# Reordering the first 20 microseconds of a fused layernorm, GLU and state-space kernel: warm-up products first, the first group's turns between grad's products, and turned x copied on ScalarE

## The chip, the cores and the metric

The kernel runs on one core of one Trainium2 chip. The metric is the device time of one execution in microseconds (us), median over several executions.

Engines: PE is TensorE (matmuls), PEld its weight loads, DVE is VectorE, ACT is ScalarE, POOL is GpSimd, SP is SyncE. PSUM is the memory that PE writes its products to and DVE and ACT read them from (in the timelines below the tiles `ps_...`: PE's rows write them, rows such as `xT<-ps_mm` on DVE and ACT read them).

The order in which each engine works through its instructions is fixed when the program is built: a scheduler orders the whole program, engine by engine, and at run time each engine takes its list from the front. So moving one call in the source can move other instructions on other engines too.

## The reference, cut to what matters

```python
# forward; the kernel returns its output and the gradients of all inputs for grad_out
x = A_u                                   # [1, 2048, 576], bfloat16
xn = layernorm(x)
gate = xn @ W_gate; up = xn @ W_up        # W: [576, 4608]
h = relu(gate) * up
out = x + S4(xn, A, B, C, log_dt, Dskip) + h @ W_down
# out, and the vector-Jacobian product of (x, A_*, B_*, C_*, log_dt, Dskip, W_*) with grad_out
```

The kernel goes through the 4608 hidden columns in 12 chunks of 384, each chunk in three units of 128 (`ft` = 0, 1, 2), and through the 2048 rows in four groups of 512 (`sg` = 0 to 3). The first chunk also normalises x. After it, the work of the state-space part (S4) is woven in between the chunks' products.

## The kernel before

Warm-up. PE multiplies an identity by itself 60 times, meant to run before any input has landed, so that PE is at its full rate when real work comes:

```python
    ps = g.psum_s4.tile([P, 512], F32, name="ps_s4")
    for i in range(WARM):                               # 60
        nc.tensor.matmul(ps[:, 0:P], lhsT=g.ident_bf[:], rhs=g.ident_bf[:], start=True, stop=True)
    nc.scalar.copy(warm[:], ps[:, 0:1])
```

Normalising one group and turning it (a "turn" is a 128x128 transpose on PE; five of them fill one PSUM tile, and one copy takes it to SBUF):

```python
def ln_group(g, pools, sg, x4, gT):
    for j in range(JS):                                 # 4 row blocks: statistics on DVE
        # ... 2 x bn_stats and 1 x bn_aggr of x4[:, j]
    # ... mean and rounding on DVE, square root (sdb) on ACT, sdf and rinv on DVE
    for j in range(JS):                                 # x - mean: DVE and ACT in turn
        # ...
    for j in range(JS):
        nc.vector.tensor_scalar(xn4[:, j, 0:D], x4[:, j, :], g.rinv[...], None, op0=ALU.mult)
        pt = g.psum_mm.tile([P, 512], F32, name="ps_mm")[:]...
        for k in range(NK):                             # 5 turns
            nc.tensor.transpose(out=pt[:, k, :], in_=xn4[:, j, k * P:(k + 1) * P], identity=g.ident_bf[:])
        (nc.vector.tensor_copy if j % 2 == 0 else nc.scalar.copy)(xT[:, :, j * P:(j + 1) * P], pt[:, 0:NK, :])
    # ... stores of xT and xn
```

The products of grad for group 0 (three bundles of five matmuls, `first`), one unit, and the order of the first chunk:

```python
    def first(self, gT):
        for ft in range(FTC):                           # 3
            ps = g.psum_mm.tile([P, 512], F32, name="ps_mm")
            # ... 5 matmuls of gT into ps
            nc.scalar.copy(self.dh0[ft], ps[:])

    def a_unit(self, c, sg, ft, turns=()):
        # gate: 5 matmuls of xT; up: 5 of xT; grad: 5 of gT (group 0 of chunk 0 has it from first)
        nc.scalar.activation(rg, ps_g[:], ACT.Relu)                                     # reads gate's PSUM tile
        nc.vector.scalar_tensor_tensor(upm, rg, 0.0, ps_u[:], op0=ALU.is_gt, op1=ALU.mult)  # reads up's
        # ... products on DVE

    # gen, chunk 0:
                xs = [ln_load(g, self.ln_sb, 0, 2)]
                # ... loads: wd[2], gT of group 0, wd[0], wd[1], x of group 1, wf, x of groups 2 and 3
                self.first(gT)
                self.X[(0, 0)] = ln(0, xs[0], gT)
                for ft in range(FTC):
                    yield from self.a_unit(0, 0, ft)
                self.X[(0, 1)] = ln(1, xs[1], self.load_gT(1))
                # ... then units of group 1, turns of group 2, products with wf, and so on
```

All of these tiles come from one PSUM pool, `psum_mm`, with five tiles; a second pool, `psum_s4`, belongs to the S4 part.

Of the kernel before, what the change touches and what calls it, by code (L numbers as in the profile page):

```python
# [10 lines left out]
F32 = mybir.dt.float32  # L11
# [3 lines left out]
P = 128  # L15
# [8 lines left out]
NK = 5  # L24
DP = NK * P
Fc = 384
FTC = Fc // P
# [43 lines left out]
def dchunks():  # L71
    return [(k, k * P, min(P, D - k * P)) for k in range(NK)]
# [4 lines left out]
def make_consts(g):  # L77
    nc, consts = g.nc, g.consts
    g.ident_bf = consts.tile([P, P], BF16, name="ident_bf")
    make_identity(nc, g.ident_bf[:])  # L80
    g.hpcol = consts.tile([P, 1], F32, name="hpcol")
    nc.vector.memset(g.hpcol[:], math.pi / 2)
    warm = consts.tile([P, 1], F32, name="warm")
    nc.scalar.activation(warm[:], g.hpcol[:], ACT.Sqrt)
    ps = g.psum_s4.tile([P, 512], F32, name="ps_s4")
    for i in range(WARM):
        nc.tensor.matmul(ps[:, 0:P], lhsT=g.ident_bf[:], rhs=g.ident_bf[:], start=True, stop=True)
    nc.scalar.copy(warm[:], ps[:, 0:1])
    g.rinv = consts.tile([P, ST], F32, name="rinv")
    g.dsk_acc = consts.tile([P, NK, NSG], F32, name="dsk_acc")  # L90

# [15 lines left out]
def ln_load(g, sb, sg, pieces=1):  # L107
    nc = g.nc
    x4 = sb.tile([P, JS, D], BF16, name="x4")
    n = JS // pieces  # L110
    for j in range(0, JS, n):
        nc.sync.dma_start(x4[:, j:j + n], g.x_v[:, sg * JS + j:sg * JS + j + n, :])
    return x4

def ln_group(g, pools, sg, x4, gT):
    nc, bal = g.nc, g.bal
    sb, small = pools
    t0 = sg * JS
    mv = small.tile([P, JS, nc.vector.BN_AGGR_DIM], F32, name="mv")
    for j in range(JS):  # L120
        stats = small.tile([P, 2, nc.vector.BN_STATS_DIM], F32, name="stats")
        for s in range(2):
            nc.vector.bn_stats(out=stats[:, s, :], in_=x4[:, j, s * DH:(s + 1) * DH])
        nc.vector.bn_aggr(out=mv[:, j, :], in_=stats[:])
    mvb = small.tile([P, JS, 2], BF16, name="mvb")
    nc.vector.tensor_copy(mvb[:], mv[:])
    veb = small.tile([P, JS], BF16, name="veb")
    nc.vector.tensor_scalar(veb[:], mvb[:, :, 1], 1e-5, None, op0=ALU.add)
    sdb = small.tile([P, JS], BF16, name="sdb")
    nc.scalar.activation(sdb[:], veb[:], ACT.Sqrt)  # L130
    neg = small.tile([P, JS], F32, name="neg")
    nc.vector.tensor_scalar(neg[:], mvb[:, :, 0], -1.0, None, op0=ALU.mult)
    sdf = small.tile([P, JS], F32, name="sdf")
    nc.vector.tensor_copy(sdf[:], sdb[:])
    nc.vector.reciprocal(g.rinv[:, t0:t0 + JS], sdf[:])
    xn4 = sb.tile([P, JS, DP], BF16, name="xn4")
    nc.gpsimd.memset(xn4[:, :, D:DP], 0.0)
    xT = g.xtp.tile([P, NK, JS * P], BF16, name="xT")
    for j in range(JS):
        if j % 2 == 0:  # L140
            nc.vector.tensor_scalar(x4[:, j, :], x4[:, j, :], neg[:, j:j + 1], None, op0=ALU.add)
        else:
            nc.scalar.activation(x4[:, j, :], x4[:, j, :], ACT.Identity, bias=neg[:, j:j + 1])
    for j in range(JS):
        nc.vector.tensor_scalar(xn4[:, j, 0:D], x4[:, j, :], g.rinv[:, t0 + j:t0 + j + 1], None, op0=ALU.mult)
        pt = g.psum_mm.tile([P, 512], F32, name="ps_mm")[:].bitcast(BF16).rearrange("p (k t) -> p k t", t=P)
        for k in range(NK):
            nc.tensor.transpose(out=pt[:, k, :], in_=xn4[:, j, k * P:(k + 1) * P], identity=g.ident_bf[:])
        (nc.vector.tensor_copy if j % 2 == 0 else nc.scalar.copy)(xT[:, :, j * P:(j + 1) * P], pt[:, 0:NK, :])
    nc.sync.dma_start(g.xT_dram[sg], xT[:])  # L150
    nc.sync.dma_start(g.xn_dram[:, t0:t0 + JS, :], xn4[:, :, 0:D])
    for k, d0, dsz in dchunks():
        nc.sync.dma_start(g.xs_dram[k][:, t0:t0 + JS, :], xn4[:, :, d0:d0 + dsz])
    bal.add(d=6.5, a=2.5)
    return xT, gT

class Ffn:
# [38 lines left out]
        nc.sync.dma_start(xT[:], g.xT_dram[sg])  # L196
        self.X[(c, sg)] = (xT, self.load_gT(sg))

    def first(self, gT):
        g, nc = self.g, self.g.nc  # L200
        for ft in range(FTC):
            ps = g.psum_mm.tile([P, 512], F32, name="ps_mm")
            for k in range(NK):
                nc.tensor.matmul(ps[:], lhsT=self.wd[2][:, k, ft * P:(ft + 1) * P], rhs=gT[:, k, :], start=(k == 0), stop=(k == NK - 1))
            self.dh0[ft] = self.op.tile([P, 2, D], BF16, name="osx")[:].rearrange("p i d -> p (i d)")[:, 0:JS * P]
            nc.scalar.copy(self.dh0[ft], ps[:])
# [158 lines left out]
    def gen(self, ln, final):  # L365
        g, lu = self.g, FTC - 1
        for c in range(NFC):
            if c == 0:
                xs = [ln_load(g, self.ln_sb, 0, 2)]
                self.load_wd(0, (2,))  # L370
                gT = self.load_gT(0)
                self.load_wd(0, (0, 1))
                xs.append(ln_load(g, self.ln_sb, 1))
                self.load_wf(0, g.nc.sync)
                xs += [ln_load(g, self.ln_sb, sg) for sg in (2, 3)]
                self.first(gT)
                self.X[(0, 0)] = ln(0, xs[0], gT)
                for ft in range(FTC):
                    yield from self.a_unit(0, 0, ft)
                self.X[(0, 1)] = ln(1, xs[1], self.load_gT(1))  # L380
            else:
                self.load_wd(c)
                self.load_x(c, 0)
                for j in range(JS):
                    yield from self.outdx(c - 1, NSG - 1, j, turns=[(c - 1, NSG - 1, lu)] if j == 0 else ())
                for q in range(4):
                    yield from self.dw_down(c - 1, q)
                self.load_wf(c)
                yield from self.a_unit(c, 0, 0)
                for i in range(4):  # L390
                    yield from self.dw_gu(c - 1, i)
                    if i % 2 == 1 and 1 + i // 2 < FTC:
                        yield from self.a_unit(c, 0, 1 + i // 2)
                yield from self.dw_left(c - 1)
                for ft in range(3, FTC):
                    yield from self.a_unit(c, 0, ft)
                if c == 1:
                    self.dskip(0)
                elif c == 2:
                    self.dskip_out()  # L400
            if c > 0:
                self.load_x(c, 1)
            late = [(c, 0, ft) for ft in range(FTC)]
            for sg in range(1, NSG):
                todo = list(range(JS))
                for ft in range(FTC):
                    n = max(1, (len(late) + lu - 1) // lu) if ft < lu else len(late)
                    turns, late = late[:n], late[n:]
                    yield from self.a_unit(c, sg, ft, turns)
                    if c == 1 and ft == lu:  # L410
                        self.dskip(sg)
                    late.append((c, sg, ft))
                    if c == 0 and ft == 0 and sg < 3:
                        self.X[(0, sg + 1)] = ln(sg + 1, xs[sg + 1], self.load_gT(sg + 1))
                    for j in todo[:JS // lu] if ft < lu - 1 else todo:
                        if ft == lu:
                            break
                        args = (c, sg - 1, j)
                        if c == NFC - 1:
                            yield "last"  # L420
                            args += (final,)
                        yield from self.outdx(*args)
                    todo = todo[JS // lu:]
                if sg < NSG - 1 and c > 0:
                    self.load_x(c, sg + 1)
                if sg == NSG - 2:
                    self.rows(c, 0)
        c = NFC - 1
        for j in range(JS):
            yield from self.outdx(c, NSG - 1, j, final, turns=[(c, NSG - 1, lu)] if j == 0 else ())  # L430
        for i in range(4):
            yield from self.dw_down(c, i)
        for i in range(4):
            yield from self.dw_gu(c, i)
        yield from self.dw_left(c)
# [784 lines left out]
```

## Time and profile before

| | before |
|---|---|
| time, median of 6 executions | 1805.13 us (1802.98 to 1808.24) |
| PE busy, share of the span | 96% |
| first product of gate (group 0) | 20.46 us |
| first product of gate (group 1) | 29.75 us |
| first product with wf (`ps_mm<-wf,T`) | 35.70 us |
| first product of the S4 part (`<-sig,Sx`) | 96.03 us |

The last two rows are landmarks, read from PE's timeline.

The line of busy times on the page of the kernel before (us, share of the span, instructions):

```profile
PE 1724.5 (96%) x16449; PEld 1188.0 (66%) x16449; DVE 1309.8 (73%) x2867; ACT 1187.4 (66%) x2736; POOL 204.3 (11%) x246
```

PE is what binds: only work or waits taken out of PE's own row can shorten the run by much, and there is 4% of waits in all.

PE's timeline in the kernel before. Columns: start, busy time in us, engine, source line, operation, output and inputs, shape, count; in brackets how long PE had been idle and what released it:

```profile
8.69 0.58 PE L204 MATMUL ps_mm<-gT,wd_152 128*128 128x512 bf16 x1 [8.69 <-DMA gT<-in_gT_dram]
9.07 5.68 PE L87 MATMUL ps_s_75<-ident_bf 128*128 128x128 bf16 x60
14.59 3.19 PE L204 MATMUL ps_mm<-gT,wd_152 128*128 128x512 bf16 x14
17.61 1.28 PE L148 MATMUL ps_mm<-ident_bf,xn_266 128*128 128x128 bf16 x20
20.46 1.24 PE L235 MATMUL ps_mm<-xT,wd_150 128*128 128x512 bf16 x5 [1.57 <-ACT xT L149]
...
29.75 1.25 PE L235 MATMUL ps_mm<-xT,wd_150 128*128 128x512 bf16 x5 [1.53 <-DVE xT L149]
...
35.70 4.57 PE L288 MATMUL ps_mm<-wf,T 128*128 128x288 bf16 x36
```

Three things are to be seen. PE does nothing until 8.69, when gT lands. The 60 warm-up products then run in front of 14 of the 15 products of grad, when real products are already there to run. (PE's rate isn't up yet. The clock column of the profile shows 1.00, so this slow beginning isn't in that column.) Between the turns (17.61) and gate's first product (20.46) PE waits 1.57 us for the turned x.

The windows of the kernel before: for each stretch the width in us and each engine's busy time, in brackets the instructions that touch the stretch; PEclk is the granted clock of PE, 1.00 is full:

```profile
core 0: us, PE busy (x) PEld busy (x) DVE busy (x) ACT busy (x) POOL busy (x), PEclk, DMA share, GB/s
...
18.00:21.00 3.00, 1.43 (x19) 1.10 (x17) 2.98 (x9) 2.41 (x5) 0.00 (x0) 1.00 0.38 135
21.00:24.00 3.00, 3.00 (x16) 1.36 (x14) 2.89 (x11) 0.70 (x2) 0.00 (x0) 1.00 0.89 290
24.00:27.00 3.00, 3.00 (x17) 1.35 (x16) 3.00 (x9) 1.09 (x2) 0.00 (x0) 1.00 0.94 210
27.00:30.00 3.00, 1.47 (x23) 1.18 (x22) 3.00 (x11) 1.69 (x4) 0.00 (x0) 1.00 0.95 294
```

### The profile page before, as it was taken

The numbers are of one execution on the slowest core, as the hardware profiler recorded it, in microseconds if no ns is written. First come the engines' busy times: TensorE is split into PE (matmuls) and PEld (weight loads), VectorE is DVE, ScalarE is ACT, GpSimd is POOL, SyncE is SP. The second block draws the span as 40 slices with busy tenths as digits, with TensorE's granted clock in tenths as the row PEclk, the third lists the DMA queues.
The fourth block names the chain that finished last, engine by engine and source line by source line (L and its number), as shares of the span: only waits on it lengthen the run. The fifth ranks groups of instructions, "written<-read, shape, count | busy, mean of one in ns | idle before, by whom it ended". The sixth has DMA issues, their size and how long they took to land. (4 is left out here: it accounts for less than half of the span.)

```text
span 1804.8 us, 42093 instructions
## 1 busy us (share of the span) xinstructions
PE 1724.5 (96%) x16449; PEld 1188.0 (66%) x16449; DVE 1309.8 (73%) x2867; ACT 1187.4 (66%) x2736; POOL 204.3 (11%) x246
## 2 busy tenths in 40 slices
PE   7989989999999999999999999999999998999998
PEld 5665557667566666766756766766676675576676
DVE  7565885677888788668777889889888863872551
ACT  5875874686577578568468657748857745864651
POOL 0200011012022012011102101101101100110000
PEclk9999999999999999999999999999999999999999
DMA  8799989679568566766857856756666578995873
GB/s 293 264 331 301 332 238 284 193 181 252 163 137 202 179 178 146 227 183 153 225 157 183 230 167 153 214 171 156 174 179 151 111 211 262 249 288 156 266 241 100
DMA packets 239004, 373.30 MB, mean 207 GB/s; under 512 B 49490, under 2 KB 153428, under 8 KB 237268
## 3 DMA queue, kind: packets, MB, share of 16 engines
q1 hardware_dynamic: 212836, 304.09, 51.9%
q0 software_dynamic: 24384, 51.92, 18.5%
q10 hardware_dynamic: 1584, 14.60, 2.3%
q8 instruction: 129, 2.11, 0.5%
q14 instruction: 71, 0.58, 0.1%
HBM read 233.10 MB, written 137.43 MB: 205 GB/s over the span
## 5 line engine op out<-in xcount | busy, mean ns | idle before, releaser
L288 PE MATMUL ps_mm<-wf,T 128*128 128x288 bf16 x3456 | 486.7, 289 | 6.9 <-DVE T L247 2.5
L288 PEld LDWEIGHTS <-T 128*128 128x128 bf16 x3456 | 325.9, 99 | 94.8 <-issue 10.1
L67 ACT CAST osx<-ps_mm 128x288 bf16<-128x288 f32 x682 | 261.2, 432 | 58.0 <-PE ps_mm L288 54.1
L301 POOL DMA_DIRECT2D acc_dram<-osx x160 | 138.0, 862 | 1054.6 <-ACT osx L67 652.3
L341 PEld LDWEIGHTS <-rows 128*128 128x128 bf16 x1536 | 145.9, 98 | 94.0 <-issue 1.8
L245 DVE SCALAR_TENSOR_TENSOR rg<-rg,ps_mm 128x512 bf16<-128x512 bf16 x144 | 98.2, 682 | 120.9 <-PE ps_mm L235 91.4
L261 PEld LDWEIGHTS <-T 128*128 128x128 bf16 x1728 | 127.6, 98 | 88.3 <-DVE T L247 7.1
L235 PE MATMUL ps_mm<-xT,wd_150 128*128 128x512 bf16 x720 | 180.0, 379 | 5.0 <-DMA xT<-xT_dram 1.7
L235 PE MATMUL ps_mm<-xT,wd_151 128*128 128x512 bf16 x720 | 180.0, 379 | 0.0
L235 PE MATMUL ps_mm<-gT,wd_152 128*128 128x512 bf16 x705 | 176.4, 379 | 0.7 <-DMA gT<-in_gT_dram 0.7
L261 PE MATMUL ps_mm<-ident_bf,T 128*128 128x128 bf16 x1728 | 157.8, 220 | 7.8 <-DVE T L247 4.3
L325 PE MATMUL ps_mm<-rows,hN 128*128 128x144 bf16 x2304 | 159.1, 227 | 0.0
L325 PEld LDWEIGHTS <-hN 128*128 128x128 bf16 x2304 | 148.5, 98 | 8.1 <-issue 5.5
L67 ACT CAST obw<-ps_mm 128x384 bf16<-128x384 f32 x103 | 49.1, 477 | 140.7 <-PE ps_mm L341 105.9
L341 PE MATMUL ps_mm<-duN,rows 128*128 128x384 bf16 x768 | 136.3, 326 | 0.0
L341 PE MATMUL ps_mm<-dgN,rows 128*128 128x384 bf16 x768 | 136.1, 326 | 0.0
L244 ACT ACTIVATE rg<-ps_mm 128x512 bf16<-128x512 f32 x144 | 87.1, 605 | 55.6 <-PE ps_mm L235 55.0
L67 ACT CAST dhb<-ps_mm 128x512 bf16<-128x512 f32 x141 | 83.7, 594 | 56.1 <-PE ps_mm L235 54.4
L252 DVE TENSOR_TENSOR T<-dhb,rg 128x1024 bf16<-128x1024 bf16 x141 | 98.5, 698 | 26.4 <-ACT dhb L67 26.3
L235 PEld LDWEIGHTS <-wd_150 128*128 128x128 bf16 x720 | 66.3, 98 | 65.1 <-issue 5.1
L235 PEld LDWEIGHTS <-wd_151 128*128 128x128 bf16 x720 | 65.0, 98 | 60.1 <-issue 2.1
L235 PEld LDWEIGHTS <-wd_152 128*128 128x128 bf16 x705 | 63.3, 98 | 57.9 <-issue 1.2
(2504 smaller groups left out, 3047.0 us busy)
## 6 DMA issues: line engine op xcount, KB each, us to landing
acc_dram<-osx POOLq DMA_DIRECT2D x176, 288.0 KB, 5.0
gT<-in_gT_dram SPq DMA_DIRECT2D x48, 640.0 KB, 6.1
xT<-xT_dram SPq DMA_DIRECT2D x44, 640.0 KB, 6.0
rows<-in_gq_dram SPq DMA_DIRECT2D x48, 576.0 KB, 4.0
wf<-in_Wf_dram ACTq DMA_DIRECT2D x11, 1296.0 KB, 8.5
ex_dram<-exs SPq DMA_DIRECT2D x36, 320.0 KB, 4.4
ex<-ex_dram SPq DMA_DIRECT2D x36, 320.0 KB, 3.7
out_dram<-obw SPq DMA_DIRECT2D x96, 96.0 KB, 2.5
```

Source lines behind the costliest of these rows:

```text
L67: self.nc.scalar.copy(out, in_)
L235: nc.tensor.matmul(ps[:], lhsT=w[:, k, fs], rhs=rhs[:, k, :], start=(k == 0), stop=(k == NK - 1))
L244: nc.scalar.activation(rg, ps_g[:], ACT.Relu)
L245: nc.vector.scalar_tensor_tensor(upm, rg, 0.0, ps_u[:], op0=ALU.is_gt, op1=ALU.mult)
L252: nc.vector.tensor_tensor(T[:, 1:3], dhb.unsqueeze(1).to_broadcast([P, 2, JS * P]), ru[:], op=ALU.mult)
L261: nc.tensor.transpose(out=pt[:, j, :], in_=src[:, j * P:(j + 1) * P], identity=g.ident_bf[:])
L288: nc.tensor.matmul(ps[:, cs], lhsT=lt, rhs=rh, start=(i == 0), stop=(i == len(mms) - 1))
L301: nc.gpsimd.dma_start(g.acc_dram[:, t, :, :], o[:], accum_op=ALU.add)
L325: nc.tensor.matmul(ps[:, ft * 144:(ft + 1) * 144], lhsT=self.hN[:, st, ft * P:(ft + 1) * P], rhs=gq[:, st, :], start=(st == 0), stop=(st = ...
L341: nc.tensor.matmul(ps[:, :Fc], lhsT=xs[:, st, 0:P], rhs=src[:, st, :], start=(st == 0), stop=(st == ST - 1))
```

## The change

The intent: use the idle time before 8.69 for the warm-up, let the turns of group 0 run as soon as x is normalised, move group 1's turns forward by one unit, and take the copies of turned x off DVE.

```diff
-    ps = g.psum_s4.tile([P, 512], F32, name="ps_s4")
+    g.ps0 = g.psum_mm.tile([P, 512], F32, name="ps_mm")
     for i in range(WARM):
-        nc.tensor.matmul(ps[:, 0:P], lhsT=g.ident_bf[:], rhs=g.ident_bf[:], start=True, stop=True)
-    nc.scalar.copy(warm[:], ps[:, 0:1])
+        nc.tensor.matmul(g.ps0[:, 0:P], lhsT=g.ident_bf[:], rhs=g.ident_bf[:], start=True, stop=True)
@@ ln_group
-        (nc.vector.tensor_copy if j % 2 == 0 else nc.scalar.copy)(xT[:, :, j * P:(j + 1) * P], pt[:, 0:NK, :])
+        (nc.vector.tensor_copy if False else nc.scalar.copy)(xT[:, :, j * P:(j + 1) * P], pt[:, 0:NK, :])
@@ first
-    def first(self, gT):
+    def first(self, gT, fts):
-        for ft in range(FTC):
-            ps = g.psum_mm.tile([P, 512], F32, name="ps_mm")
+        for ft in fts:
+            ps = g.psum_mm.tile([P, 512], F32, name="ps_mm") if ft > 0 else g.ps0
@@ gen, chunk 0
-                self.first(gT)
+                self.first(gT, (0,))
                 self.X[(0, 0)] = ln(0, xs[0], gT)
+                self.first(gT, range(1, FTC))
                 for ft in range(FTC):
+                    if ft == FTC - 1:
+                        self.X[(0, 1)] = ln(1, xs[1], self.load_gT(1))
                     yield from self.a_unit(0, 0, ft)
-                self.X[(0, 1)] = ln(1, xs[1], self.load_gT(1))
```

The warm-up writes the PSUM tile that the first real product writes next. So nothing can put that product ahead of the warm-up any more.

## The prediction

> **What bounds the kernel.** PE. The page's busy table has PE 1724.5 us of 1804.8 (96%), DVE 73%, ACT 66%, clock full throughout. So a change gains only what it takes out of PE's order or waits; this one touches the first 60 us.
>
> **The opening, from the timeline.** PE waits until 8.69 us for gT (PE's largest single wait, 8.7 us). The first product of grad runs, then, although written first in the program, the 60 warm-up products: 9.07 to 14.59. In the windows table they run 12 per us (about 83 ns each) until about 13.5, then 25 to 30 per us. The other 14 products of grad follow (14.59 to 17.6, 216 ns each), the 20 turns of group 0 (17.6 to 18.9, 60 to 65 ns each), a wait of 1.57 us for the turned x, and gate and up begin at 20.46. The wait is ACT's: casts of grad (0.58 us) and biases of group 1 (0.76, 0.79) stand between its copies of xT (0.70).
>
> **What the change does.**
> 1. The warm-up shares a PSUM tile with the first real product, so it must come first. ident_bf is ready at 1.6 us; 60 products at 83 ns fill 1.8 to about 6.8, inside the wait for gT. Off the critical path: about -5.5 us.
> 2. Group 0's turns come after five products of grad; normalised x is ready at 9.70 (DVE timeline). Estimate: five products 8.7 to 9.8, turns to 11.1, ten products to 13.2. Four copies on ACT (about 0.65 each in a row) and a cast end near 13.1. Gate and up start at 13.2 instead of 20.46. With 1: -7.2 us.
> 3. Group 1's turns move before the last gate/up unit: the 1.53 us wait before 29.75 can go, but xn of group 1 may not be ready by 17.5 (its x lands at 12.46): net -0.5 us.
> 4. Copies: eight go from DVE (0.48) to ACT (0.70): ACT +5.6, DVE -3.9 us. ACT is 97% busy in 30 to 40 us, so groups 2 and 3 may stall PE: +0.5 us.
> 5. DMA is full from 8.7 to 18 us (about 400 GB/s) and 90 to 100% busy from 25 to 60. gT of group 1 and later tiles are wanted 8 us earlier against the same bytes: +1 us.
> 6. Clock: [...] the rate doubles some 5 us after the first product. [...]
>
> The rest is the same work in nearly the same order; static reordering may move it a few us either way.
>
> **Prediction.** 1805.1 - 7.7 + 2 = about 1799.4 us, 8 in 10 within 1794.5 to 1804.5. Faster by over 2%: 0.01; within 2%: 0.98; slower: 0.01.
>
> **What would show it.** Warm-ups end before 8 us; first gate product near 13.2, unit (group 1, first) near 22 instead of 29.75; PE busy down by only 0 to 1 us, with the gain in idle before the first gate product; DVE busy -4, ACT +5.
>
> **What would make it wrong.** The scheduler reordering later stages; the lead eaten by DMA waits (gT, xT) before 100 us; cold products at the start.

How the sum was made: steps 1 to 3 give -7.2 - 0.5 = -7.7 us, and the +2 was 0.5 (step 4) + 1 (step 5) + 0.5 for the clock (step 6), which gave 1799.4. The clock's term and its reason are cut from step 6, because no trace or run of this case shows the reason; without the term the sum is 1805.1 - 7.7 + 1.5 = 1798.9. "Clock full throughout" was read from the page, whose clock row has 9 (90% or more) in all 40 slices; over that whole run the mean granted clock is 0.992. "Cold products" means products at PE's slow rate, as the first warm-up products above.

## More of the kernel before

DVE is nearly full from 18 us (2.89 to 3.00 of 3), and in 27 to 30 it's busy 3.00 of 3 us while PE isn't.

Landmarks come from one profile of each kernel. The landing of gT, a load at the very start, varies and moves what follows it, so differences of less than about 1 us between two landmarks shouldn't be leaned on.

## The result, and the profile after

| | before | after |
|---|---|---|
| time, median | 1803.49 us of 20 (1797.64 to 1813.49) | 1802.98 us of 10 (1800.88 to 1813.23) |
| gate, group 0 | 20.46 us | 12.95 us |
| gate, group 1 | 29.75 us | 27.35 us |
| first product with wf | 35.70 us | 34.60 us |
| first product of S4 | 96.03 us | 95.34 us |

The ratio is 1.0002, 95% interval 0.9985 to 1.0019: the same. A ratio here is the mean time of one kernel's fast runs over the mean of the other's in the same rounds, so it isn't quite the ratio of the medians in the table (and the 6 executions of the first table are among these 20).

So 7.51 us were won at the gate, as predicted, and 0.7 us were left at 95 us. Nearly all of it was given back between 12.95 and 34.60.

The line of busy times of the kernel after:

```profile
PE 1726.3 (96%) x16449; PEld 1186.8 (66%) x16449; DVE 1307.1 (72%) x2859; ACT 1191.5 (66%) x2743; POOL 205.0 (11%) x246
```

PE's busy time rose by 1.8 us although the work is the same; DVE fell by 2.7 and ACT rose by 4.1, somewhat less than the predicted 4 and 5.

PE's timeline in the kernel after:

```profile
1.66 4.79 PE L87 MATMUL ps_mm<-ident_bf 128*128 128x128 bf16 x60 [1.66 <-POOL ident_bf masks.py:199]
8.60 1.24 PE L203 MATMUL ps_mm<-gT,wd_151 128*128 128x512 bf16 x5 [2.15 <-DMA gT<-in_gT_dram]
...
12.95 1.24 PE L234 MATMUL ps_mm<-xT,wd_149 128*128 128x512 bf16 x5
...
16.19 1.24 PE L234 MATMUL ps_mm<-xT,wd_150 128*128 128x512 bf16 x5
19.31 0.73 PE L147 MATMUL ps_mm<-ident_bf,xn_376 128*128 128x128 bf16 x10 [1.87 <-ACT rg L243]
21.17 1.02 PE L147 MATMUL ps_mm<-ident_bf,xn_376 128*128 128x128 bf16 x10 [1.13 <-DVE rg L244]
23.13 2.29 PE L234 MATMUL ps_mm<-xT,wd_149 128*128 128x512 bf16 x5 [0.94 <-DVE rg L244]
25.22 2.34 PE L234 MATMUL ps_mm<-xT,wd_150 128*128 128x512 bf16 x5
27.35 1.69 PE L234 MATMUL ps_mm<-xT,wd_149 128*128 128x512 bf16 x5
...
32.96 1.59 PE L147 MATMUL ps_mm<-ident_bf,xn_532 128*128 128x128 bf16 x20 [0.42 <-DVE xn_532 L144]
34.60 4.88 PE L287 MATMUL ps_mm<-wf,T 128*128 128x288 bf16 x36
```

To be read against the one of before: the warm-up is at 1.66 and done before gT lands at 8.60; gate begins at 12.95. Then PE waits three times (1.87 and 1.13 us at the turns of group 1, and 0.94 before the last unit). The named releasers are `rg`, that is, the instructions of the units that read PSUM (`relu` on ACT, L243, and the product on DVE, L244). And the five-product bundles at 23.13 and 25.22 are busy for 2.29 and 2.34 us where such a bundle took 1.24 at 16.19.

The windows of the kernel after tell why the bundles are slow (columns as above):

```profile
core 0: us, PE busy (x) PEld busy (x) DVE busy (x) ACT busy (x) POOL busy (x), PEclk, DMA share, GB/s
...
18.00:21.00 3.00, 0.73 (x10) 0.66 (x11) 3.00 (x12) 2.47 (x5) 0.00 (x0) 1.00 1.05 386
21.00:24.00 3.00, 1.89 (x13) 1.17 (x13) 3.00 (x9) 1.37 (x3) 0.00 (x0) 0.57 1.08 227
24.00:27.00 3.00, 3.00 (x9) 1.04 (x8) 1.97 (x7) 0.60 (x1) 0.00 (x0) 0.50 1.00 324
27.00:30.00 3.00, 3.00 (x19) 1.45 (x18) 2.33 (x9) 0.87 (x2) 0.00 (x0) 0.79 1.10 351
```

From 21 us on the granted clock is 0.57, 0.50 and 0.79. In finer slices it is exactly one half from about 21.4 to 28.2 us. In the profile of before it is 1.00 in all the windows shown above. Note also DVE: 3.00 of 3 in 21 to 24, and 1.97 and 2.33 in the two windows of slow products, since then DVE waits for PE (1.70 us in one piece, until 27.66).

What DVE and ACT did before that, from the timeline of all engines in the kernel after (a few of its rows):

```profile
17.66 0.46 DVE L122 BATCH_NORM_STATS2 stats<-x_209 128x6 f32<-128x288 bf16 x1 [0.66 <-DMA x_209<-in_A_u_dram]
...
18.20 1.07 ACT L243 ACTIVATE rg<-ps_mm 128x512 bf16<-128x512 f32 x2
...
18.89 1.20 DVE L144 TENSOR_SCALAR xn_376<-x_206,rinv 128x576 bf16<-128x576 bf16 x4
...
20.44 0.68 DVE L244 SCALAR_TENSOR_TENSOR rg<-rg,ps_mm 128x512 bf16<-128x512 bf16 x1
...
22.39 0.69 DVE L244 SCALAR_TENSOR_TENSOR rg<-rg,ps_mm 128x512 bf16<-128x512 bf16 x1
```

At 17.66 DVE takes up a statistics instruction on x_209, which is group 2's x; it waited 0.66 us for that to land. Group 1's normalised x (`xn_376`), for which PE has been waiting since 17.4, comes behind it, at 18.89 (the first of its four blocks is done at about 19.3, the last at 20.09). The trace puts PE's first wait down to a relu on ACT that ends at 19.27, but that is the same moment, and in e11 below, where the turns need no tile of the units, the same wait ends with the normalised x. So the first wait counts as one for DVE. The two DVE products that free the units' PSUM tiles come at 20.44 and 22.39, and it is those that release the second half of the turns (21.17) and the last unit (23.13).

The ledger from gate's first product to wf's first product: 35.70 - 20.46 = 15.24 us before, 34.60 - 12.95 = 21.65 us after, 6.41 more. Of this:

- waits: 1.87 + 1.13 + 0.94 + 0.42 = 4.36 against 1.53, so 2.83 more;
- units at half clock: the 15 products from 23.13 to 28.88 took 5.75 us; at full clock they take 15 x 0.216 = 3.24 (in this trace such products start 216 ns apart at full clock and 427 ns at half); so 2.51 more;
- group 1's turns: 0.73 + 1.02 against 1.28, so 0.47 more, of which about 0.3 is half clock (in e5 the second half takes 0.72 at full clock);
- the rest, 0.6 us, is spread: 0.27 of it in group 2's turns (1.59 against 1.32).

The first product of S4, PE's timeline before:

```profile
96.03 0.29 PE L609 MATMUL ps_s_1560<-sig,Sx 128*128 128x288 bf16 x1
```

and after:

```profile
95.34 0.29 PE L610 MATMUL ps_s_1558<-sig,Sx 128*128 128x288 bf16 x1
```

The lead of 1.1 us at 34.60 is 0.7 us here. So it isn't in later stages that most of the gain goes; of 7.5 us, 6.4 are gone before 35 us.

### The profile page after: what moved, and what is told of

It is laid out like the page before. It is cut to its first block, busy times and chain, and to the rows that moved or that the text cites. A ratio compares the mean times of both kernels' runs of the same rounds, so it can differ in the third digit from the quotient of the medians.

```text
span 1803.0 us, 42088 instructions
## 1 busy us (share of the span) xinstructions
PE 1726.3 (96%) x16449; PEld 1186.8 (66%) x16449; DVE 1307.1 (72%) x2859; ACT 1191.5 (66%) x2743; POOL 205.0 (11%) x246
## 5 line engine op out<-in xcount | busy, mean ns | idle before, releaser
L244 DVE SCALAR_TENSOR_TENSOR rg<-rg,ps_mm 128x512 bf16<-128x512 bf16 x144 | 98.3, 682 | 120.3 <-PE ps_mm L234 89.9
L243 ACT ACTIVATE rg<-ps_mm 128x512 bf16<-128x512 f32 x144 | 87.1, 605 | 53.7 <-PE ps_mm L234 53.1
```

## The experiments

Theories on the table, in words: the new waits of group 1's turns took the gain, and half the clock came from them; the copies on ACT took it; VectorE's work for later groups held group 1 back; the landings of x in memory order did; the units' PSUM tiles, being held, did. Twelve kernels ran (the record has no number 10). "wf" is the start of the first product with wf, "S4" that of the first S4 product.

| kernel | gate | wf | S4 | half clock in 8 to 35 us | median us | ratio to before (95%) |
|---|---|---|---|---|---|---|
| before | 20.46 | 35.70 | 96.03 | none | 1803.49 | 1 |
| after | 12.95 | 34.60 | 95.34 | 21.4 to 28.2 | 1802.98 | 1.0002 (0.9985 to 1.0019) |
| e1_move_undone | 13.70 | 34.52 | 95.24 | 24.8 to 31.6 | 1802.59 | 0.9994 (0.9975 to 1.0013) |
| e2_dve_copies | 17.98 | 34.19 | 94.52 | 9.9 to 13.3 | 1800.52 | 0.9987 (0.9964 to 1.0011) |
| e3_warm_only | 19.75 | 37.40 | 97.72 | 16.9 to 23.7 | 1805.12 | 1.0012 (0.9989 to 1.0034) |
| e4_fill | 13.64 | 36.86 | 97.59 | none | 1805.86 | 1.0014 (0.9994 to 1.0034) |
| e5_no_stats | 12.95 | 34.52 | 95.26 | 22.6 to 29.4 | 1806.77 | 0.9988 (0.9956 to 1.0019) |
| e6_fused | 13.16 | 32.65 | 93.07 | none | 1801.03 | 0.9969 (0.9947 to 0.9990) |
| e7_x3_late | 13.41 | 34.06 | 97.26 | 21.0 to 27.8 | 1806.46 | 0.9998 (0.9979 to 1.0016) |
| e8_before_x3_late | 20.64 | 36.10 | 99.38 | none | 1810.58 | 1.0022 (0.9997 to 1.0047) |
| e9_x2_before_wf | 12.95 | 34.74 | 95.47 | 22.6 to 29.4 | 1803.46 | 1.0001 (0.9976 to 1.0025) |
| e11_turns_s4 | 12.94 | 32.34 | 92.80 | 20.2 to 23.6 | 1801.30 | 0.9991 (0.9968 to 1.0013) |
| e12_combined | 12.48 | 35.88 | 96.38 | 25.3 to 32.1 | 1804.14 | 1.0002 (0.9980 to 1.0025) |
| e13_gT_early | 13.80 | 32.69 | 93.15 | none | 1798.69 | 0.9987 (0.9963 to 1.0011) |

No total is over 2% from before, and all but one interval (that of e6, which isn't a valid kernel) include 1. The landmarks are what tells the theories apart; the totals can only confirm.

### e1: the move of group 1's turns undone

Against the kernel after:

```diff
                 for ft in range(FTC):
-                    if ft == FTC - 1:
-                        self.X[(0, 1)] = ln(1, xs[1], self.load_gT(1))
                     yield from self.a_unit(0, 0, ft)
+                self.X[(0, 1)] = ln(1, xs[1], self.load_gT(1))
```

> The changed kernel with one part undone: group 1's turns are called again after the three units of group 0. Theory W (waits): the lead of 7.5 us that the changed kernel has at its first gate product (12.95 against 20.46) is spent by group 1's turns, which stand in PE's order before the last unit at a time when their x is not normalised and PSUM is not free (1.87 + 1.13 + 0.94 us of PE waits), and by the half clock that these waits bring on (21.6 to 28.2 us, about 2.5 us). W expects here: last unit follows at once (by 19.0), first gate product of group 1 at 22 to 24 (changed: 27.35, before: 29.75), no half clock between 15 and 30, first product with wf at 29 to 31.5 (changed: 34.60), and a total 3 to 6 us below before at equal clock. Rival C (copies): the loss is the turned x of all groups on ACT; then nothing is regained. Rival D (later stage sets the pace): the lead is taken back by other waits before 60 us, so the first L-product of the fourth stage at about 95 us stays within 1 us of 95.3.

Measured: gate at 13.70 (gT landed later, at 9.35), the turns of group 1 at 21.26 and 23.22 after waits of 0.43 and 1.25 us for the same DVE products, then 1.77 us for the copied xT, and half clock from 24.8 on. wf starts at 34.52, against 34.60. My expectation that the lead would be kept failed. The waits move behind the units and are as long; the place of the turns isn't the cause by itself.

### e2: copies alternate between DVE and ACT again

Against the kernel after:

```diff
-        (nc.vector.tensor_copy if False else nc.scalar.copy)(xT[:, :, j * P:(j + 1) * P], pt[:, 0:NK, :])
+        (nc.vector.tensor_copy if j % 2 == 0 else nc.scalar.copy)(xT[:, :, j * P:(j + 1) * P], pt[:, 0:NK, :])
```

> The changed kernel with the copies of turned x alternating between DVE and ACT again, in all four groups; warm-up and moves stay. Rival C expects the lead back: first wf product near 30 and 4 us less in all. Theory W expects the waits at group 1's turns as in the changed kernel (first gate product of group 1 within 1.5 us of 27.35) and a total within 2 us of it.

Measured: a DVE copy of xT then stands behind group 1's statistics, PE waits 1.97 us for it, and gate starts at 17.98, five us later than in the kernel after. wf nevertheless starts 0.4 us earlier (34.19). Not all of these five us are the copies': gT landed 1.24 us later in this profile (9.84 against 8.60), and the first products of grad and group 0's turns ran at half clock (9.9 to 13.3, a loss of up to 1.7 us), after PE had idled 2.37 us behind the early warm-up. So the copies on ACT bring about 2 us at the gate, and giving them up doesn't bring the lead back at wf. What they cost there isn't told by the 0.4 us, since e2 also lost less to half clock than the kernel after. The main lesson is another: five us at the gate were worth nothing at wf. What sets wf's time is not when gate begins.

### e3: the warm-up alone moved ahead

Against the kernel before:

```diff
-    ps = g.psum_s4.tile([P, 512], F32, name="ps_s4")
+    g.ps0 = g.psum_mm.tile([P, 512], F32, name="ps_mm")
     for i in range(WARM):
-        nc.tensor.matmul(ps[:, 0:P], lhsT=g.ident_bf[:], rhs=g.ident_bf[:], start=True, stop=True)
-    nc.scalar.copy(warm[:], ps[:, 0:1])
+        nc.tensor.matmul(g.ps0[:, 0:P], lhsT=g.ident_bf[:], rhs=g.ident_bf[:], start=True, stop=True)
@@ first
-            ps = g.psum_mm.tile([P, 512], F32, name="ps_mm")
+            ps = g.psum_mm.tile([P, 512], F32, name="ps_mm") if ft > 0 else g.ps0
```

> The kernel before with the warm-up alone forced ahead (shared PSUM tile), nothing moved, copies alternating. Theory W: first gate product at 14 to 15 us (5.5 to 6.5 us ahead of before), group 1's first gate product at 23 to 24.5 (before: 29.75), total 3 to 6 us below before at equal clock. Rival D: lead gone by 60 us, total as before. Rival K (clock): an earlier warm-up by itself lets the array fall to half clock in 15 to 30 us; then the granted clock there is under 0.9 here too.

Rows of the timeline of all engines in e3 (columns as before):

```profile
12.63 1.18 DVE L122 BATCH_NORM_STATS2 stats<-x 128x6 f32<-128x288 bf16 x3 [2.82 <-DMA x<-in_A_u_dram]
...
18.11 0.88 DVE L148 COPY xT<-ps_mm 128x640 bf16<-128x640 bf16 x2
18.43 1.27 ACT L148 COPY xT<-ps_mm 128x640 bf16<-128x640 bf16 x2
...
19.75 0.59 PE L234 MATMUL ps_mm<-xT,wd 128*128 128x512 bf16 x1 [6.40 <-ACT xT L148]
```

PE was done with the turns of group 0 at 13.3 and then waited 6.40 us. The copies on DVE (18.11) and ACT (18.43) stand behind most of the normalisation of group 1, whose x landed at 12.63. So step 1 of the prediction, the warm-up out of the way, is worth 0.7 us at the gate alone, not 5.5: behind the 60 products the next in-order queue was already the limit. It takes step 2 (turns earlier, copies on ACT) to get 7.5. Wf came later than before (37.40). Part of that is clock: PE ran at half clock from 16.9 to 23.7.

### e4: unused products put into the new waits

Against the kernel after, inside `ln_group` (the results are thrown away; each `fill` reads the data whose arrival should time it):

```diff
+    def fill(n, rhs):
+        pf = g.psum_s4.tile([P, 512], F32, name="ps_s4")
+        for i in range(n):
+            nc.tensor.matmul(pf[:, 0:P], lhsT=g.ident_bf[:], rhs=rhs, start=True, stop=True)
     for j in range(JS):
+        if sg == 1 and j == 0:
+            fill(30, x4[:, 0, 0:P])
+        if sg == 1 and j == 2:
+            fill(16, xn4[:, 1, 0:P])
@@ after the loop
+    if sg == 1:
+        fill(14, xn4[:, 3, 0:P])
```

> The changed kernel with 60 extra products of 128 columns, results unused, placed in PE's order inside its three waits at group 1's turns (30 before the turns, 16 between second and third turn, 14 after the fourth). It splits waits from clock. Theory W: the waits stay (last unit starts at 23 to 24 as in the changed kernel), but the clock stays full from 20 to 30 us, so last unit and the next product take 3.3 us and not 5.7; first wf product at 32 to 33 instead of 34.60. Rival K: half clock appears between 20 and 30 all the same.

PE's timeline in e4 (L146 are the unused products):

```profile
17.96 1.84 PE L146 MATMUL ps_s<-x,ident_bf 128*128 128x128 bf16 x30
...
20.28 1.06 PE L146 MATMUL ps_s<-xn,ident_bf 128*128 128x128 bf16 x16
...
22.12 0.94 PE L146 MATMUL ps_s<-xn,ident_bf 128*128 128x128 bf16 x14
23.54 3.40 PE L244 MATMUL ps_mm<-xT,wd 128*128 128x512 bf16 x14 [0.47 <-DVE rg L254]
26.77 0.61 PE L270 MATMUL ps_mm<-ident_bf,T 128*128 128x128 bf16 x8
28.98 1.24 PE L244 MATMUL ps_mm<-xT,wd 128*128 128x512 bf16 x5 [1.59 <-ACT rg L253]
...
36.86 1.37 PE L297 MATMUL ps_mm<-wf,T 128*128 128x288 bf16 x8
```

No half clock: the bundle of units from 23.54 on takes 3.23 us to 26.77 (15 products, of which 14 are recorded), against 5.75 in the kernel after. That the clock fell because of the waits is supported by this one profile: the waits filled, it stays (all 14 traces together, below, show it better). But wf starts at 36.86, 2.3 us later than after. New waits follow (1.59 at 28.98, and 0.76, 1.06 and 0.71 later), all for DVE and ACT: in e4's static order the third unit's product on DVE came behind statistics of groups 2 and 3. So the clock was not the only bound; with it whole, DVE's order bound instead.

### e5: no statistics for groups 2 and 3 (wrong result)

Against the kernel after:

```diff
-    for j in range(JS):
+    if sg >= 2:
+        nc.gpsimd.memset(mv[:], 0.0025)
+    for j in range(JS if sg < 2 else 0):
         stats = small.tile([P, 2, nc.vector.BN_STATS_DIM], F32, name="stats")
```

> Wrong result on purpose: the changed kernel without the mean and variance instructions of groups 2 and 3 (16 of 0.41 us and 8 of 0.2 us on DVE); their moments are set to a constant. Theory V, formed after the first four runs, where no version kept the lead: from the landing of group 1's x at 12.4 us DVE works without a break on the normalisation of groups 1 to 3 and on the units, and PE waits for what DVE yields (normalised x, freed PSUM). V expects here: group 1's normalised x by 18.7 instead of 20.1, its turns about 1.5 us earlier, first wf product at 30.5 to 33 (changed: 34.60), and 1.5 to 4 us less in all at equal clock. If ACT or the transfers set the pace instead, first wf product stays within 1 us of 34.6.

Measured: DVE still stops for 0.97 us at 18.12, for the landing of a later group's x, now with the subtraction of the mean in the statistics' place; the turns start at 19.40 (19.31 after), half clock from 22.6, wf at 34.52 (34.60). The theory expected the freed time to help, and it didn't: without 16 statistics instructions nothing came sooner. But it isn't refuted as a whole: the scheduler moved other work on the later groups into the room, and DVE was nearly as busy from 18 to 24 us as in the kernel after (5.84 of 6 us against 6.00). What is seen in the trace is the order, one instruction on data that isn't there yet, ahead of work on data that is.

### e6: x normalised by one instruction instead of two

Against the kernel after (skips one rounding to bfloat16):

```diff
-        if j % 2 == 0:
-            nc.vector.tensor_scalar(x4[:, j, :], x4[:, j, :], neg[:, j:j + 1], None, op0=ALU.add)
-        else:
-            nc.scalar.activation(x4[:, j, :], x4[:, j, :], ACT.Identity, bias=neg[:, j:j + 1])
-    for j in range(JS):
-        nc.vector.tensor_scalar(xn4[:, j, 0:D], x4[:, j, :], g.rinv[...], None, op0=ALU.mult)
+        nc.vector.tensor_scalar(xn4[:, j, 0:D], x4[:, j, :], neg[:, j:j + 1], g.rinv[...], op0=ALU.add, op1=ALU.mult)
```

> The changed kernel with normalisation in one DVE instruction (add, then multiply) instead of an add (half on DVE, half on ACT) and a multiply; it skips one rounding. It takes about 2.6 us from DVE and 6.2 us from ACT in the opening. Theory V: first gate product a little earlier only if x was late (it was not: gT is), group 1's turns 0.7 to 1.5 us earlier, first wf product 1 to 3 us before 34.60, total 1 to 3 us below the changed kernel at equal clock. If PE's own order were the bound, nothing moves.

Measured: the turns start at 19.47, hardly changed, but the waits after them are shorter (0.82 and 0.60 against 1.13 and 0.94), there is no half clock in this profile, and wf starts at 32.65, 3.05 before the kernel before. Its result was wrong, with a relative error of 0.043 in one output (`out[10]`, the gradient of W_gate), so it isn't a candidate. It shows that the lead can be kept; that ACT and DVE freed PSUM sooner and that the clock held are both seen in its trace, and their shares aren't told apart.

### e7 and e8: x of group 3 loaded later

The same edit, e7 against the kernel after and e8 against the kernel before:

```diff
-                xs += [ln_load(g, self.ln_sb, sg) for sg in (2, 3)]
+                xs.append(ln_load(g, self.ln_sb, 2))
@@ where the later groups are normalised
                         self.X[(0, sg + 1)] = ln(sg + 1, xs[sg + 1], self.load_gT(sg + 1))
+                        if sg == 1:
+                            xs.append(ln_load(g, self.ln_sb, 3))
```

> The changed kernel with the load of group 3's x issued only after group 2's turns, so that its mean and variance leave DVE's order before the first wf product. Theory V expects little here, 0 to 1.5 us, because the changed kernel's DVE has gaps after 25 us (3.3 of 5 us busy) and group 3's instructions stand there; its waits at group 1's turns are from group 2's x.

> The kernel before with the same late load of group 3's x and nothing else. Before is where DVE is full from 18 to 37 us. Theory V expects the wait of 1.53 us for turned x before 29.75 to shrink and first wf product at 33 to 35 (before: 35.70), with 1 to 2.5 us less in all at equal clock, although PE's opening with the warm-up in its way is untouched. If PE's opening is the bound in before, first wf product stays at 35.7.

Measured in e7: turns at 20.33, half clock from 21.0, wf at 34.06, then a later wait, and S4 at 97.26. In e8: wf at 36.10, later than before (35.70), S4 at 99.38. The gain expected of e8 failed, and the little that e7 has at wf (0.5 us) is lost by S4. The load that was put off is wanted later and costs 2 to 3 us there. Little was learned of the cause, except that taking group 3's data away from DVE's list isn't enough.

### e9: x of group 2 loaded ahead of wf

Against the kernel after:

```diff
                 xs.append(ln_load(g, self.ln_sb, 1))
+                xs.append(ln_load(g, self.ln_sb, 2))
                 self.load_wf(0, g.nc.sync)
-                xs += [ln_load(g, self.ln_sb, sg) for sg in (2, 3)]
+                xs.append(ln_load(g, self.ln_sb, 3))
```

> The changed kernel with the load of group 2's x moved ahead of the load of wf. In the changed kernel, and in the runs without statistics and with fused normalisation, DVE's order has an instruction on group 2's x ahead of the last steps of group 1's normalisation, and it waits there for that x to land at 17.7 to 18.1 us; group 1's turns start at 19.3 to 19.5 in all of them. Theory M (queue order behind a landing): with group 2's x landing at 14 to 15 us the wait is gone. M expects group 1's normalised x 0.5 to 1.5 us earlier, turns from 18.0 to 19.0, first wf product 33 to 34.5. If the turns still start at 19.3, the landing was not what held them.

Measured: turns at 20.12, later and not sooner, wf at 34.74. With group 2's x there earlier, the scheduler puts more of group 2's statistics ahead of group 1's normalised x. So the landing of that load isn't the cause alone either: the static order fills the room it's given.

### e11: group 1's turns in the other PSUM pool

Against the kernel after:

```diff
-        pt = g.psum_mm.tile([P, 512], F32, name="ps_mm")[:]...
+        pt = (g.psum_s4.tile([P, 512], F32, name="ps_s4") if sg == 1 else g.psum_mm.tile([P, 512], F32, name="ps_mm"))[:]...
```

> The changed kernel with group 1's turned blocks written to PSUM of the other pool, which lies unused in the opening, so that they need no bank that the units hold until DVE and ACT have read it. Theory S (PSUM held by slow readers): the waits of 1.13 and 0.94 us inside and behind the turns go, the turns run 19.3 to 20.6, the last unit starts at 20.3 to 21.5 (changed: 23.13), group 1's first gate product at 23 to 24.5, first wf product at 31 to 33.5 (changed: 34.60), half clock shorter or absent. If the units' own evictions are the bound, the wait only moves to the last unit and first wf product stays within 1 us of 34.6.

PE's timeline in e11:

```profile
19.62 1.31 PE L147 MATMUL ps_s<-ident_bf,xn 128*128 128x128 bf16 x15 [2.21 <-DVE xn L144]
20.73 0.63 PE L234 MATMUL ps_mm<-xT,wd 128*128 128x512 bf16 x1
21.16 0.74 PE L147 MATMUL ps_s<-ident_bf,xn 128*128 128x128 bf16 x5
21.70 4.12 PE L234 MATMUL ps_mm<-xT,wd 128*128 128x512 bf16 x14
...
32.34 4.62 PE L287 MATMUL ps_mm<-wf,T 128*128 128x288 bf16 x36
```

The turns still wait 2.21 us for `xn`, but once they run, 15 of the 20 go in one stretch, the last unit's first product comes in the middle (20.73) instead of at 23.13, and wf starts at 32.34: 2.3 us sooner than in the kernel after and 3.4 sooner than before. The half clock lasts 3.4 us instead of 6.8, which is 1.7 us of these 2.3; the waits from gate to wf sum to 3.94 us against 4.36. In the source the edit changes nothing but where the turned x is put. So the second and third waits of the kernel after were waits for PSUM tiles held by the units' readers, as its releasers said; taking them away paid mostly by the clock. New waits came (0.83 us for gT of group 1, 0.90 for group 2's normalised x).

### e12: several edits at once

The move undone as in e1, group 1's turns in the other pool as in e11, x of group 2 before wf as in e9, and the copies of groups 2 and 3 alternating:

```diff
-        (nc.vector.tensor_copy if False else nc.scalar.copy)(xT[:, :, j * P:(j + 1) * P], pt[:, 0:NK, :])
+        (nc.vector.tensor_copy if sg >= 2 and j % 2 == 0 else nc.scalar.copy)(xT[:, :, j * P:(j + 1) * P], pt[:, 0:NK, :])
```

> A candidate to beat both: the changed kernel with group 1's turns behind the three units again (as in the first run), written to the other PSUM pool, group 2's x loaded ahead of wf, and the copies of groups 2 and 3 alternating between DVE and ACT. If the lead is lost to the order, to the landing and to held PSUM, all three are lifted here: PE runs the three units without a gap to 19.5, turns to 20.7, group 1's gate at 21 to 23, first wf product at 29 to 31.5, and the total 5 to 8 us below before at equal clock. If DVE's work from 12.4 us on is the bound as such, first wf product stays above 32 and the total within 4 us of before.

Measured: wf at 35.88, worse than any part. That pool has three tiles, group 1 has four; the fourth waits 4.98 us for the first copy on ACT, which stands in ACT's list behind relus and mean subtractions that themselves wait for DVE. Good parts don't add where every edit gives a new order.

### e13: e11 and gT of group 1 loaded earlier

Against e11:

```diff
                 xs += [ln_load(g, self.ln_sb, sg) for sg in (2, 3)]
+                gT1 = self.load_gT(1)
                 self.first(gT, (0,))
@@
-                        self.X[(0, 1)] = ln(1, xs[1], self.load_gT(1))
+                        self.X[(0, 1)] = ln(1, xs[1], gT1)
```

> The run with group 1's turns in the other PSUM pool, and also the load of group 1's gT issued ahead of group 0's stores, since PE waited 0.83 us for that gT there. Expected: that wait goes, first wf product at 31.3 to 32.3 (32.34 without it), the lead over before at that product 3.4 to 4.4 us and kept within 0.5 us until the first product of the fourth stage (96.03 in before). In total 1 to 4 us below before; a clear verdict is not expected, because half-clock periods move single executions by several us. If the transfers are the bound, the stores of group 0 pushed back by this load hold up something else and the product is later than 32.4.

Measured: the wait for gT is gone and there is no half clock, but gate starts later (13.80, gT of group 0 landed at 9.45) and DVE waits of 1.08, 0.83 and 1.16 us came in its place; wf at 32.69, so the expected gain over e11 was missed (here gT of group 0 had landed 0.86 us later than in e11). Its median, 1798.69, is the lowest of all valid kernels. Its ratio, 0.9987 (0.9963 to 1.0011), isn't clear of 1.

### All executions together: what the spread is

The executions list the mean granted clock of each. I fitted one line through 115 executions of the 14 kernels: each kernel its own level, one common slope. The result: time = level + 1949 (standard error 152) us x (1 - mean granted clock). The residual is 2.1 us, where single executions of one kernel spread by 3.4 (standard deviations, pooled). So a good part of the spread between executions of one kernel is clock, and a difference of 0.001 in the mean clock is 1.9 us.

| kernel | S4 landmark against before, us | half clock in the opening, clock loss, us | landmark without that loss, us | level at equal clock against before, us (standard error) | mean clock |
|---|---|---|---|---|---|
| before | 0 | 0 | 0 | 0 | 0.9930 |
| after | -0.7 | 3.4 | -4.1 | -2.3 (0.7) | 0.9916 |
| e1 | -0.8 | 3.4 | -4.2 | -3.8 (0.9) | 0.9918 |
| e2 | -1.5 | 1.7 | -3.2 | -5.7 (0.9) | 0.9915 |
| e3 | +1.7 | 3.4 | -1.7 | -0.8 (0.9) | 0.9920 |
| e4 | +1.6 | 0 | +1.6 | +2.4 (0.9) | 0.9932 |
| e5 | -0.8 | 3.4 | -4.2 | -2.5 (1.2) | 0.9905 |
| e6 | -3.0 | 0 | -3.0 | -3.8 (1.1) | 0.9925 |
| e7 | +1.2 | 3.4 | -2.2 | -1.5 (1.1) | 0.9910 |
| e8 | +3.4 | 0 | +3.4 | +5.2 (1.1) | 0.9923 |
| e9 | -0.6 | 3.4 | -4.0 | -3.1 (0.9) | 0.9915 |
| e11 | -3.2 | 1.7 | -4.9 | -3.1 (0.9) | 0.9925 |
| e12 | +0.4 | 3.4 | -3.0 | -2.8 (0.9) | 0.9915 |
| e13 | -2.9 | 0 | -2.9 | -2.6 (0.9) | 0.9937 |

(The clock loss is the length of the half-clock period times one half, since products start 427 ns apart in it and 216 ns at full clock. The fourth column is the second less the third.) The fourth column is from one profile each, the fifth from all executions and the whole span. They agree within 2 us but for e2, where 2.5 us stay unexplained. (The loss is the most that the period can cost; it costs less where PE waits anyway.) So what a version has at 95 us, apart from its opening's clock, is about what it has at the end: the later stages neither give nor take much.

The mean clocks go with the opening's half clock too, over all executions and not only the profiled ones: the five kernels whose profile shows none have 0.9923 to 0.9937, the seven with 6.8 us of it 0.9905 to 0.9920.

When did the clock fall? In the traces its changes lie on a grid of 3.41 us (in the kernel after at 4.36 us and multiples of 3.41 from there), and the half-clock periods of the opening last 3.41 us (e2, e11) or 6.83 us (after, e1, e3, e5, e7, e9, e12), one or two steps of it. I cut the 14 traces at their own grids and took PE's busy time in each window, turns included. In the opening (windows that end between 8 and 37 us) the clock was full in 97. Behind the nine with 0.00 to 1.45 us of work it fell to one half: in the kernel after 18.01 to 21.43 with 1.00 us, and one window each of e1, e2, e3, e5, e7, e9, e11 and e12. Behind the other 88, with 1.50 us or more, it stayed full. Also in the opening, it came back after a window with 3.19 us or more and not after one with 2.47 or less. So in these openings the falls came behind windows that PE's waits had left with little work, and with the waits filled (e4) there was none. How the waits lie on the grid tells: e6 and e13, without half clock, have windows of 1.58 and 1.71 us at group 1's turns, and in e1 the clock stayed up over a single wait of 2.94 us (6.41 to 9.35). The turns belong in the sum: in the kernel before the clock stayed up behind a window (17.03 to 20.44) with 1.86 us of work, 0.74 of products and 1.28 of turns that overlap a little, while in e2 it fell behind one (6.50 to 9.91) with 1.04 us of products and no turns. Over the whole of the traces of before and after, from PE's first product on, the border is less sharp: of the windows at full clock it fell behind all 11 with under 1.40 us, behind 4 of 21 from there to 2.0, and behind none of 1004 with more.

For the change itself: at equal clock it gains 2.3 us; its mean clock is 0.0013 lower (0.99164 against 0.9930), which costs 0.0013 x 1949 = 2.6 us; the net is about nothing, as measured. The opening's half-clock period alone, 3.4 us of 1803, would make 0.0019.

## Why the prediction was right or wrong

The time lay in the range (1802.98 in 1794.5 to 1804.5) and the class was right, but the predicted gain of 6 us did not come. That the time lay in the range says little for the mechanism: a kernel without any change would have lain in it too (before has 1803.49 in the same rounds). Point by point, as the prediction put it:

1. "Off the critical path: about -5.5 us", and "With 1: -7.2 us" for steps 1 and 2: right in sum, -7.51 at the gate (12.95 against an expected 13.2). The split is wrong. By e3 the warm-up's own share is 0.7 us. The 83 ns per product were misread too: the window counts count a product on both sides of a boundary; by start times it was 107 ns, then 56, and the 60 took 4.79 us in the kernel after.
2. "Gate and up start at 13.2 instead of 20.46": right. What was wrong is the unsaid step from here to the total, that a lead at the gate is a lead at the end. e2 gave up five us at the gate and lost nothing at wf.
3. "net -0.5 us" for group 1's turns: this is the step that failed. The prediction did doubt that group 1's x would be ready by 17.5; it comes from 18.89 on, with the first block at about 19.3. Measured between gate and wf: waits of 4.36 us against 1.53, so +2.8 in place of -0.5. I counted the landing of x and not the instruction on group 2's x that stands ahead in DVE's list, nor the PSUM tiles that the units hold until ACT and DVE have read them. e11 shows the PSUM part (2.3 us at wf, of which 1.7 by shorter half clock); the order on DVE is seen in the trace, and e5, e7 and e9 failed to remove it.
4. "+0.5 us" for the copies on ACT: not confirmed. The one wait in the place named, 0.42 at 32.96 before the turns of group 2, is for the normalised x from DVE, and e2, with the copies back on DVE, has it too (0.48 and 0.28). Neither is e2's 0.4 us at wf a measure of it.
5. "+1 us" for DMA: too much. Over the whole run the waits of the unit products for gT changed from 0.7 to 0.9 us, and between 8.60 and 34.60 no wait of PE in the kernel after ended with a DMA. Indirectly it did tell: the landing of group 2's x held DVE for 0.66 us at 17.66.
6. The clock's +0.5 (the author's estimate, cut above): mis-sized, and the loss came in another place than the one feared. The worry was the warm-up; at 8.60 the products ran at full clock in this profile (216 ns apart), while in e2 the first products ran at half clock, from 9.9 to 13.3. The loss came at 21.4 to 28.2, behind the waits of step 3 (1.87 and 1.13 us): 2.5 us on the units and about 0.3 on turns. That is one fall in one profile; the busy times of the windows above show the same link behind all nine falls of the openings.

"What would make it wrong" named cold products "at the start", and lost lead to DMA; neither was it in the profile of the kernel after. The signs named as tests: the warm-up before 8 us was right, first gate product right, DVE -4 and ACT +5 nearly (-2.7, +4.1). "Unit (group 1, first) near 22" was wrong (27.35), and that's the row where the failure can be read off at once. "PE busy down by 0 to 1 us" was wrong in sign: up 1.8. The unit products with xT, which met the opening's half clock, took 2.8 us more, others less.

What stays open: what else sets the start of the first wf product. The shares of DVE's order, of ACT and of the landings weren't separated, as each edit gives a new static order on every engine. Whether e11 or e13 is really faster than the kernel before (about 3 us at equal clock) isn't decided by their totals. Why e2's level at equal clock is 2.5 us lower than its landmark says isn't known.

## What to carry to other kernels

A gain on one engine's path is worth what the next in-order queue lets through (here 7.51 us at the gate were 1.10 at wf): before costing a move, look for what its inputs and its output tiles wait for at the new time, and read the order of the other engines' lists there, not only the landing of the data. A row that gets ahead of its suppliers gains waits, and here PE's waits of 1.87 and 1.13 us, with turns alone between them, were followed by half the clock for 6.8 us; so ask of every saving on PE where the idle time will be afterwards. When the effect is of some tenths of a per cent, compare landmarks in the traces and times at equal granted clock; the medians alone can't tell.
